# Reordering the first four units of a fused linear attention and FFN: operands of the bonus product, masks, and the release of row transfers

## Chip, cores and metric

The kernel runs on one core of a Trainium2 chip. The time is device microseconds of the whole launch; a run of it is compared with runs of the other kernel on the same chip.

## What is computed

The reference has two stages. The first is a linear attention with a decaying state for 4 batches, 8 heads, 768 steps and a head width of 48. The second is an FFN with a SiLU that takes the attention's output as 3072 tokens of 384 columns.

```python
for t in range(S):
    cur = np.einsum('bhd,bhe->bhde', u[None] * kt, vt)
    y[:, :, t] = np.einsum('bhd,bhde->bhe', rt, state + cur)
    state = w[None, :, :, None] * state + np.einsum('bhd,bhe->bhde', kt, vt)
x = y.transpose(0, 2, 1, 3).reshape(B * S, H * D)
h = x @ w_in                       # 384 -> 2048
out = (h / (1 + exp(-h))) @ w_out  # 2048 -> 384
```

All inputs and the output are float32. The decay w lies between 0.85 and 0.95 for each head and column.

## The kernel before

The 768 steps are cut into six chunks of 128, so with four batches there are 24 units (`unit`: chunk, batch). Units 0 to 3 are the first chunk of the four batches, 4 to 7 the second, and so on. Each unit loads r, k and v as 128 steps by 8 heads by 48 columns of float32 (192 KB, `ld`, line 71, on the queue of SyncE). The tiles `rin`, `kin`, `vin` have eight buffers each. The heads of r and k are padded from 48 to 64 columns of zero, by VectorE for the first four buffers and by ScalarE in `pads` for the other four.

A unit goes through these steps, named as in the order string:

- `T`: TensorE transposes r and k into a PSUM tile (`att`, two of them used in turn), line 251. `rT`, `kT`: VectorE multiplies by powers of the decay, line 257.
- `A01`, `A23`, ...: `product_pair`, line 284, the products of the decayed k and r for two units.
- `am`: VectorE masks these, line 291 (`maskM` for even units, `maskX` for odd ones).
- `ku`, `ru`, `rd`, `vu`: the term with u. GpSimd forms k*u (line 211), r*(k*u) (line 215), VectorE sums over the columns of a head (line 224), and GpSimd multiplies v by the sum (line 229).
- `v16`: ScalarE casts v, with two more copies for odd units (lines 238 to 242). `kc`: GpSimd decays k for the state (line 219). `r16`: cast of the decayed r for units of later chunks.
- `Y`, `S`: TensorE's products for the output and the state (lines 306, 318). `y16`: VectorE adds vu (line 334). `st`, `sd`, `stb`: state, its decay and its half-precision copy.
- `yT`, `xT`: TensorE turns the output, ScalarE copies it into `xT` (lines 372, 376), the input of the FFN. From unit 6 on a DMA transpose does that.
- `L`, `G` and `H`: pieces of the first FFN matmul and its SiLU (lines 387, 395). `L0.4` is the piece of batches 0 and 1 that begins at block 4 of 16 of the 2048 columns, `L2.` that of batches 2 and 3, `L4.` those of all four. The second FFN matmul is at line 408.
- `i_q0` to `i_q3`, `i_o0` to `i_o3`: requests of a quarter of `w_in` and `w_out`, on GpSimd's queue (lines 84, 89). They cast to half precision on the way. `i_q0` holds blocks 0 to 3, and so on.
- `lr`, `lk`, `lv`: loads of r, k, v of a unit. A number ahead of a star, as in `4*T0`, puts so many filler matmuls (`spin`, line 161) ahead of a step on TensorE.

Nothing reorders the program: each engine runs its instructions in the order in which they are written, with a semaphore wait where data or a buffer isn't ready. For units 0 to 5 and part of 6 and 7 the order is written out by hand in the string `order` (lines 485 to 496), after the loads of units 0 to 3 (lines 103 to 115). The loads of units 4 to 7 stand at the string's beginning, those of units 8 and 9 behind it. After that a loop (line 518) takes two units at a time and puts pieces of the FFN between their steps (`fill`); here the term with u is formed by `bonus_products`.

Of the kernel before, what the change touches and what calls it, by code (L numbers as in the profile page):

```python
# [8 lines left out]
FP = mybir.dt.float32  # L9
F16 = mybir.dt.float16  # L10
AF = mybir.ActivationFunctionType
ALU = mybir.AluOpType
# [3 lines left out]
def kernel(  # L16
# [11 lines left out]
    nc = tc.nc  # L28

    B, H, S, D = r.shape  # L30
# [10 lines left out]
    NIN = 8  # L41
# [4 lines left out]
    wrk = ctx.enter_context(tc.tile_pool(name="wrk", bufs=2))  # L46
# [3 lines left out]
    def unit(i):  # L50
        return divmod(i, B)
# [9 lines left out]
    u_bc = cst.tile([128, H, D], FP)  # L61
    rin = [big.tile([128, H, 64], FP, name=f"rin{i}") for i in range(NIN)]
    kin = [big.tile([128, H, 64], FP, name=f"kin{i}") for i in range(NIN)]
    vin = [big.tile([128, H, D], FP, name=f"vin{i}") for i in range(NIN)]
    kc = [big.tile([128, H, 64], F16, name=f"kc{i}") for i in range(NIN)]
    st = [big.tile([PR, NP, PW], FP, name=f"st{b}") for b in range(B)]
# [4 lines left out]
    def ld(i, dst, src, eng=nc.sync):  # L71
        sc, b = unit(i)
        eng.dma_start(
            out=dst[i % NIN][:, :, 0:D],
            in_=src[b, :, sc * C:sc * C + C, :].rearrange("h t d -> t h d"))

    def load(i):
        if i >= NU:
            return
        for dst, src in ((rin, r), (kin, k), (vin, v)):  # L80
            ld(i, dst, src)
# [29 lines left out]
                                            ap=[[0, 128], [D, H], [1, D]]))  # L111
    ld(0, vin, v)
    ld(1, vin, v)
    load(2)
    load(3)
    nc.vector.memset(ones, 1.0)
    for i in range(B):
        nc.vector.memset(rin[i][:, :, D:64], 0.0)
# [1 line left out]
    for b in range(B):  # L120
# [13 lines left out]
        out=maskM, in_=maskM, compare_op=ALU.is_ge, fill=0.0,  # L134
# [10 lines left out]
    eK = cst.tile([PR, NP, C], FP)  # L145
    lamR = cst.tile([PR, NP, C], FP)
    lamK = cst.tile([PR, NP, C], FP)
    lnw_bc = cst.tile([128, HD], FP)
    lamC = cst.tile([128, H, D], FP)
    wCT = cst.tile([PR, NP], FP)  # L150

    def pads():
        for i in range(B, NIN):
            for dst in (rin, kin):
                nc.scalar.copy(out=dst[i][:, :, D:64],
                               in_=idle[:, 0:128].rearrange("p (h d) -> p h d", h=H))

    def spin(n):
        zs = ps.tile([128, 512], FP, name="zs", tag="moe", bufs=4)
        for _ in range(n):  # L160
            nc.tensor.matmul(zs, idle[:, 0:128], idle, start=True, stop=True)
# [40 lines left out]
    def L(i):  # L202
        return live.setdefault(i, {})

    def bonus_products(i):
        bonus_ku(i)
        bonus_rku(i)

    def bonus_ku(i):
        L(i)["ku"] = wrk.tile([128, H, D], FP, name="ku")  # L210
        nc.gpsimd.tensor_tensor(out=L(i)["ku"], in0=kin[i % NIN][:, :, 0:D], in1=u_bc, op=ALU.mult)  # L211

    def bonus_rku(i):
        L(i)["rku_f"] = wrk.tile([128, H, D], FP, name="rku_f")
        nc.gpsimd.tensor_tensor(out=L(i)["rku_f"], in0=rin[i % NIN][:, :, 0:D], in1=L(i)["ku"],  # L215
                                op=ALU.mult)

    def decayed_k(i):
        nc.gpsimd.tensor_tensor(out=kc[i % NIN][:, :, 0:D], in0=kin[i % NIN][:, :, 0:D],  # L219
# [246 lines left out]
    def piece(word, f):  # L466
# [4 lines left out]
        "lnw": powers_r, "eK": exponents_k, "lamK": powers_k,  # L471
        "wb": spread_w,
        "lnwb": ln_w, "lamC": powers_c, "mx": cross_mask, "pads": pads, "clear": clear,
    }
    unit_steps = {
# [2 lines left out]
        "am": masked, "v16": cast_v, "kc": decayed_k,  # L478
        "vu": bonus_v,
        "Y": outputs_y, "S": outputs_s, "y16": evict_y, "yT": turn_y, "xT": copy_x,  # L480
        "st": state, "stb": state16, "ku": bonus_ku, "ru": bonus_rku, "rd": bonus_sum,
        "r16": cast_r, "sd": decayed_state, "i_q": ld_win, "i_o": ld_wout,
        "lr": lambda i: ld(i, rin, r), "lk": lambda i: ld(i, kin, k), "lv": lambda i: ld(i, vin, v),
    }
    order = """
        lnw eK lamK mx clear lr4 lk4 lv4 lr5 lk5 lv5 lr6 lk6 lv6 lr7 lk7 lv7 4*T0 ku0 rT0 kT0
        1*T1 rT1 kT1 v160 ru0 rd0 ku1 v161 3*A01 wb ru1 am0 rd1 vu0 lnwb i_q0 lamC pads am1 vu1
        4*Y0 y160 T2 kT2 2*Y1 y161 ku2 ru2 rT2 yT0 xT0 i_q1 yT1 xT1 v162 T3 kT3 rT3 ku3 ru3 rd2
        v163 4*A23 vu2 i_q2 rd3 vu3 am2 am3 L0.0 G0.0 L0.2 G0.2 Y2 y162 Y3 y163 kc0 yT2 xT2 L0.4
        G0.4 kc1 yT3 xT3 L0.6 G0.6 S0 st0 kc2 T4 kT4 rT4 kc3 L2.0 G2.0 S1 L2.2 G2.2 st1 ku4 v164  # L490
        L2.4 G2.4 S2 L2.6 G2.6 st2 ru4 i_q3 r164 L4.8 G4.8 S3 L4.9 G4.9 st3 rd4 ku5 L4.10 G4.10
        T5 kT5 rT5 L4.11 G4.11 vu4 ru5 i_o0 A45 rd5 am4 r165 v165 L4.12 G4.12 vu5 kc4 L4.13
        G4.13 am5 sd4 kc5 Y4 S4 y164 st4 L4.14 G4.14 sd5 i_o1 Y5 S5 y165 st5 L4.15 G4.15 yT4 xT4
        yT5 xT5 T6 kT6 rT6 ku6 ru6 i_o2 H0 H1 v166 r166 H2 H3 T7 kT7 rT7 ku7 i_o3 v167 r167 H4
        ru7 rd6 stb4 stb5
    """
    for word in order.split():
        if "*" in word:
# [19 lines left out]
    for i in range(B + 2, NU, 2):  # L518
# [3 lines left out]
        if i > B + 2:  # L522
            for n in nxt:
                bonus_products(n)
                decayed_k(n)
        if i > B + 2:
            masked(i)
            masked(i + 1)
        else:
            bonus_v(i)  # L530
            decayed_k(i)
            decayed_state(i)
            masked(i)
            bonus_sum(i + 1)
            masked(i + 1)
            bonus_v(i + 1)
            decayed_k(i + 1)
            decayed_state(i + 1)
            for n in nxt:
                bonus_products(n)  # L540
                decayed_k(n)
# [60 lines left out]
```

## Time and profile before

| | |
|---|---|
| median of 7 runs | 195.01 us (194.65 to 197.19) |
| profiled execution, its time | 194.78 us |
| its span, first to last instruction | 193.1 us |
| mean granted clock of TensorE | 0.991 |
| busy: PE, PEld | 184.1, 118.1 us |
| busy: DVE, ACT, POOL | 102.8, 108.3, 120.3 us |
| filler matmuls before the loop | 18 |

PE is TensorE's matmuls, PEld its weight loads, DVE VectorE, ACT ScalarE, POOL GpSimd, SP SyncE. A line of the timeline has the start in us, the duration, the engine, the line of the program, the operation, and out<-in with the shapes; in brackets stand the idle time before it and what ended it. A line of a stage has its bounds, its length, and the busy time of each engine with the number of instructions, then the granted clock as a fraction, the mean busy share of the DMA engines and GB/s. In the page, one digit stands for one of 40 equal slices of the span, 4.83 us each.

### The profile page before, as it was taken

The page shows a single profiled execution, that of the slowest core. Times are in us where ns is not written, and L with a number is a line of the kernel's source. Part 1 is how long each engine was busy: PE and PEld are TensorE (multiplying, and loading weights), DVE is VectorE, ACT ScalarE, POOL GpSimd, SP SyncE. Part 2 cuts the span into 40 slices and gives each one's busy share as a digit, 9 for nine tenths or more (in the row PEclk, how much of TensorE's full clock was granted, in tenths as well). Part 3 has the DMA queues.
Part 4 walks back from the last instruction along what each step waited for, and adds up shares of the span by engine and source line. Part 5 has one row for each costly group of instructions (what it writes and reads, how often), then busy time and mean ns, then how long its engine had stood idle before and what let it go on. Part 6 is the DMA issues. An engine that isn't in the chain of part 4 may idle for free.

```text
span 193.1 us, 5626 instructions
## 1 busy us (share of the span) xinstructions
PE 184.1 (95%) x2306; PEld 118.1 (61%) x2306; DVE 102.8 (53%) x188; ACT 108.3 (56%) x212; POOL 120.3 (62%) x159
## 2 busy tenths in 40 slices
PE   7888899989999999999999999999999999999994
PEld 2544684667766886665556665566655656644563
DVE  6577769764782682672672673673574364200120
ACT  5398277759371493076792176791376781089300
POOL 8299994999999939929829839839837430000000
PEclk9996999999999999999999999999999999999999
DMA  5999979899949559249259278177287101320022
GB/s 99 208 186 164 229 139 182 130 206 220 186 112 176 176 112 196 65 106 208 58 106 202 64 158 192 25 138 171 61 179 171 40 5 44 82 81 0 3 81 82
DMA packets 90267, 24.35 MB, mean 126 GB/s; under 512 B 83329, under 2 KB 90242, under 8 KB 90242
## 3 DMA queue, kind: packets, MB, share of 16 engines
q1 hardware_dynamic: 85136, 20.59, 49.2%
q0 software_dynamic: 3712, 3.15, 10.8%
q10 hardware_dynamic: 1394, 0.26, 0.7%
q8 instruction: 18, 0.29, 0.7%
q14 instruction: 7, 0.06, 0.1%
HBM read 20.65 MB, written 4.72 MB: 131 GB/s over the span
## 4 chain that ended last, share of the span: by engine, by line
PE 76%; POOL 12%; issue 4%; DMA 3%; ACT 2%; SPq 1%; DVE 1%; POOLq 0%
PE ops L408 31%; PE hps L387 27%; PE att L284 7%; PE att L251 4%; POOL ku L211 3%; POOL kc L219 3%; DMA u_bc<-in_u_dram 3%; POOL rku_f L215 2%; POOL vu L229 2%; PE yp L306 2%; PE yp L301 2%; POOL win L84 2%; PE sp L318 1%; PE ops L433 1%; ACT gT L395 1%
## 5 line engine op out<-in xcount | busy, mean ns | idle before, releaser
L387 PE MATMUL hps<-xT,win 128*128 128x512 f16 (+1 forms) x360 | 68.2, 337 | 0.7 <-ACT xT L376 0.5
L395 ACT ACTIVATE gT<-hps 128x512 f16<-128x512 f32 x96 | 56.2, 598 | 20.9 <-PE hps L387 18.8
L408 PE MATMUL ops<-wout,gT 128*128 128x384 f16 x368 | 64.0, 326 | 0.0
L408 PEld LDWEIGHTS <-gT 128*128 128x128 f16 x368 | 34.6, 98 | 22.2
L387 PEld LDWEIGHTS <-win 128*128 128x128 f16 x360 | 33.2, 98 | 24.3 <-issue 1.1
L229 POOL TENSOR_TENSOR vu<-vin,rku 128x384 f32<-128x384 f32 x24 | 19.8, 830 | 27.0 <-DVE rku L224 27.0
L414 ACT COPY osb<-ops 128x384 f32<-128x384 f32 x20 | 9.6, 478 | 43.4 <-PE ops L408 43.4
L291 DVE TENSOR_TENSOR am<-att,maskM 128x1024 f16<-128x1024 f32 x12 | 14.7, 1224 | 32.2 <-PE att L284 32.2
L211 POOL TENSOR_TENSOR ku<-kin,u_bc 128x384 f32<-128x384 f32 x24 | 24.1, 1005 | 4.9 <-DMA u_bc<-in_u_dram 3.3
L215 POOL TENSOR_TENSOR rku_f<-rin,ku 128x384 f32<-128x384 f32 x24 | 24.1, 1003 | 1.7
L219 POOL TENSOR_TENSOR kc<-kin,lamC 128x384 f16<-128x384 f32 x24 | 23.9, 1000 | 0.0
L284 PEld LDWEIGHTS att<-rT,kT 48*64 48x64 f32 x768 | 17.8, 134 | 6.5 <-issue 3.9
L257 DVE TENSOR_TENSOR rT<-att,lamR 112x512 f32<-112x512 f32 x24 | 16.4, 685 | 9.6 <-ACT gT L395 4.0
L284 PE MATMUL att<-rT,kT 48*64 48x128 f32 (+1 forms) x768 | 20.2, 248 | 1.0 <-DVE rT L257 0.8
L334 DVE TENSOR_TENSOR y<-yp,vu 128x384 f16<-128x384 f32 x24 | 13.3, 556 | 13.6 <-issue 4.8
L257 DVE TENSOR_TENSOR kT<-att,lamK 112x512 f32<-112x512 f32 x24 | 16.4, 682 | 4.1 <-PE att L251 4.1
L291 DVE TENSOR_TENSOR am<-att,maskX 128x1024 f16<-128x1024 f32 x12 | 14.6, 1214 | 0.0
L224 DVE TENSOR_REDUCE rku<-rku_f 128x8 f32<-128x384 f32 x24 | 12.4, 544 | 3.6 <-POOL rku_f L215 3.6
L238 ACT CAST v<-vin 128x384 f16<-128x384 f32 x24 | 11.4, 511 | 3.4 <-DMA vin<-in_v_dram 3.3
L329 POOL TENSOR_TENSOR sdec<-st,wCT 112x384 f32<-112x384 f32 x16 | 13.2, 825 | 0.0
L272 ACT CAST rT<-rT 112x512 f16<-112x512 f32 x20 | 12.4, 619 | 0.3 <-DVE rT L257 0.2
L306 PEld LDWEIGHTS <-am 128*128 128x128 f16 x192 | 9.7, 97 | 4.4 <-DVE am L291 2.9
(64 smaller groups left out, 161.7 us busy)
## 6 DMA issues: line engine op xcount, KB each, us to landing
rin<-in_r_dram SPq DMA_DIRECT2D x24, 192.0 KB, 4.2
vin<-in_v_dram SPq DMA_DIRECT2D x24, 192.0 KB, 4.1
kin<-in_k_dram SPq DMA_DIRECT2D x23, 192.0 KB, 4.1
out_dram<-osb SPq DMA_DIRECT2D x23, 192.0 KB, 2.2
win<-in_moe_w_in_dram POOLq DMA_DIRECT2D x4, 384.0 KB, 6.9
wout<-in_moe_w_out_dram POOLq DMA_DIRECT2D x4, 384.0 KB, 6.3
xT<-y SPq DMA_TRANSPOSE x18, 2.3
kin<-in_k_dram ACTq DMA_DIRECT2D x1, 192.0 KB, 4.0
```

What stands on the lines that cost most here:

```text
L211: nc.gpsimd.tensor_tensor(out=L(i)["ku"], in0=kin[i % NIN][:, :, 0:D], in1=u_bc, op=ALU.mult)
L215: nc.gpsimd.tensor_tensor(out=L(i)["rku_f"], in0=rin[i % NIN][:, :, 0:D], in1=L(i)["ku"], op=ALU.mult)
L219: nc.gpsimd.tensor_tensor(out=kc[i % NIN][:, :, 0:D], in0=kin[i % NIN][:, :, 0:D], in1=lamC, op=ALU.mult)
L229: nc.gpsimd.tensor_tensor(out=L(i)["vu"], in0=vin[i % NIN], in1=L(i)["rku"].unsqueeze(2).broadcast_to([128, H, D]), op=ALU.mult)
L257: nc.vector.tensor_tensor(out=L(i)[key].rearrange("p g (y t) -> p y g t", y=2), in0=L(i)["t"][0:PR, :, x], in1=lam.rearrange("p g (y t) -> ...
L284: nc.tensor.matmul(a[e][o0:o0 + HC, j, p, c0:C], kT[r0:r0 + D, p, s0:s0 + HC], rT[r0:r0 + D, p, c0:C], start=True, stop=True)
L291: nc.vector.tensor_tensor(out=am.rearrange("p h g c -> p (h g) c"), in0=L(i)["a"].rearrange("p h g c -> p (h g) c"), in1=(maskX if crossed ...
L306: nc.tensor.matmul(L(i)["y"][:, h, :], L(i)["am"][:, j, p, :], L(i)["vy"][:, h, :], start=not sc, stop=(not sc or j == 1))
L334: nc.vector.tensor_tensor(out=L(i)["y16"], in0=L(i)["y"], in1=L(i)["vu"], op=ALU.add)
L387: nc.tensor.matmul(hps[:, f, :], win[:, q, (ft + f) * 128:(ft + f + 1) * 128], xts[sc][:, q, b0:b0 + nb, :].rearrange("p b t -> p (b t)"), ...
L395: nc.scalar.activation(out=gts[sc][:, ft:ft + m, b0 * C:(b0 + nb) * C], in_=hpss[b0, ft], func=AF.Silu)
L408: nc.tensor.matmul(opss[b], gts[sc][:, ft, b * C:(b + 1) * C], wout[:, ft, :], start=(ft == 0), stop=(ft == NFT - 1))
```

## The change

1. The term with u of every unit is formed as r*k first and that times u afterwards. Both products stay on GpSimd. In the order string `ku` becomes `rk`.
2. In the prologue, r and k of units 2 and 3 are requested ahead of v of units 2 and 3.
3. The order of the first four units is written anew. `rk0 rk1 ru0 ru1` come first on GpSimd; `am0` stands ahead of `rd1`; `vu1` stands ahead of `i_q0`; `rT2` stands ahead of `y161`; T3 and A23 stand ahead of `yT1`; `v162`, `v163` and `pads` stand ahead of `xT1`; `i_q2` comes behind `kc0`. The 18 fillers are dealt out differently.
4. The loads of units 4 to 7 leave the string's beginning. Each unit's three loads are now behind a small GpSimd memset into the buffer that r will fill (`hold_rows`), so that the first of them waits until GpSimd has come that far. The holds stand behind `i_q0` (by way of `rk2` and `ru2`), `i_q2`, `i_q3` and `i_o0`.

```diff
-    load(2)
-    load(3)
+    for dst, src in ((rin, r), (kin, k)):
+        ld(2, dst, src)
+    for dst, src in ((rin, r), (kin, k)):
+        ld(3, dst, src)
+    ld(2, vin, v)
+    ld(3, vin, v)
...
+    def hold_rows(i):
+        nc.gpsimd.memset(rin[i][:, :, 0:4], 0.0)
...
-        nc.gpsimd.tensor_tensor(out=L(i)["ku"], in0=kin[i % NIN][:, :, 0:D], in1=u_bc, op=ALU.mult)
+        nc.gpsimd.tensor_tensor(out=L(i)["rk"], in0=kin[i % NIN][:, :, 0:D],
+                                in1=rin[i % NIN][:, :, 0:D], op=ALU.mult)
...
-        nc.gpsimd.tensor_tensor(out=L(i)["rku_f"], in0=rin[i % NIN][:, :, 0:D], in1=L(i)["ku"],
-                                op=ALU.mult)
+        nc.gpsimd.tensor_tensor(out=L(i)["rku_f"], in0=L(i)["rk"], in1=u_bc, op=ALU.mult)
...
-        lnw eK lamK mx clear lr4 lk4 lv4 lr5 lk5 lv5 lr6 lk6 lv6 lr7 lk7 lv7 4*T0 ku0 rT0 kT0
-        1*T1 rT1 kT1 v160 ru0 rd0 ku1 v161 3*A01 wb ru1 am0 rd1 vu0 lnwb i_q0 lamC pads am1 vu1
-        4*Y0 y160 T2 kT2 2*Y1 y161 ku2 ru2 rT2 yT0 xT0 i_q1 yT1 xT1 v162 T3 kT3 rT3 ku3 ru3 rd2
-        v163 4*A23 vu2 i_q2 rd3 vu3 am2 am3 L0.0 G0.0 L0.2 G0.2 Y2 y162 Y3 y163 kc0 yT2 xT2 L0.4
-        G0.4 kc1 yT3 xT3 L0.6 G0.6 S0 st0 kc2 T4 kT4 rT4 kc3 L2.0 G2.0 S1 L2.2 G2.2 st1 ku4 v164
-        L2.4 G2.4 S2 L2.6 G2.6 st2 ru4 i_q3 r164 L4.8 G4.8 S3 L4.9 G4.9 st3 rd4 ku5 L4.10 G4.10
-        T5 kT5 rT5 L4.11 G4.11 vu4 ru5 i_o0 A45 rd5 am4 r165 v165 L4.12 G4.12 vu5 kc4 L4.13
...
+        lnw eK lamK mx clear 4*T0 rk0 rT0 kT0 1*T1 rT1 kT1 rk1 ru0 rd0 v160 v161 3*A01 wb am0
+        ru1 vu0 rd1 am1 vu1 lnwb lamC i_q0 1*Y0 y160 T2 kT2 rT2 2*Y1 rk2 1*yT0 xT0 ru2 hold4 lr4
+        lk4 lv4 3*T3 kT3 rT3 v162 y161 rk3 i_q1 3*A23 v163 pads yT1 xT1 ru3 rd2 vu2 rd3 vu3 am2
+        am3 L0.0 G0.0 L0.2 G0.2 Y2 y162 Y3 y163 kc0 i_q2 hold5 lr5 lk5 lv5 yT2 xT2 L0.4 G0.4 kc1
+        yT3 xT3 L0.6 G0.6 S0 st0 kc2 T4 kT4 rT4 kc3 L2.0 G2.0 S1 L2.2 G2.2 st1 rk4 v164 L2.4
+        G2.4 S2 L2.6 G2.6 st2 ru4 i_q3 hold6 lr6 lk6 lv6 r164 L4.8 G4.8 S3 L4.9 G4.9 st3 rd4 rk5
+        L4.10 G4.10 T5 kT5 rT5 L4.11 G4.11 vu4 ru5 i_o0 hold7 lr7 lk7 lv7 A45 rd5 am4 r165 v165
...
```

From `L4.12` on the string is the same, but for `rk` in the place of `ku`.

More of the change, by code (lines that the diff above doesn't have):

```diff
@@ L205, in bonus_products, with bonus_rk @@
     def bonus_products(i):
-        bonus_ku(i)
+        bonus_rk(i)
         bonus_rku(i)
-    def bonus_ku(i):
-        L(i)["ku"] = wrk.tile([128, H, D], FP, name="ku")
-        nc.gpsimd.tensor_tensor(out=L(i)["ku"], in0=kin[i % NIN][:, :, 0:D], in1=u_bc, op=ALU.mult)
+    def bonus_rk(i):
+        L(i)["rk"] = wrk.tile([128, H, D], FP, name="rk")
+        nc.gpsimd.tensor_tensor(out=L(i)["rk"], in0=kin[i % NIN][:, :, 0:D],
+                                in1=rin[i % NIN][:, :, 0:D], op=ALU.mult)
     def bonus_rku(i):
         L(i)["rku_f"] = wrk.tile([128, H, D], FP, name="rku_f")
-        nc.gpsimd.tensor_tensor(out=L(i)["rku_f"], in0=rin[i % NIN][:, :, 0:D], in1=L(i)["ku"],
-                                op=ALU.mult)
+        nc.gpsimd.tensor_tensor(out=L(i)["rku_f"], in0=L(i)["rk"], in1=u_bc, op=ALU.mult)
     def decayed_k(i):
@@ L480 @@
         "Y": outputs_y, "S": outputs_s, "y16": evict_y, "yT": turn_y, "xT": copy_x,
-        "st": state, "stb": state16, "ku": bonus_ku, "ru": bonus_rku, "rd": bonus_sum,
-        "r16": cast_r, "sd": decayed_state, "i_q": ld_win, "i_o": ld_wout,
+        "st": state, "stb": state16, "rk": bonus_rk, "ru": bonus_rku, "rd": bonus_sum,
+        "r16": cast_r, "sd": decayed_state, "i_q": ld_win, "i_o": ld_wout, "hold": hold_rows,
         "lr": lambda i: ld(i, rin, r), "lk": lambda i: ld(i, kin, k), "lv": lambda i: ld(i, vin, v),
@@ L485 @@
     order = """
-        lnw eK lamK mx clear lr4 lk4 lv4 lr5 lk5 lv5 lr6 lk6 lv6 lr7 lk7 lv7 4*T0 ku0 rT0 kT0
-        1*T1 rT1 kT1 v160 ru0 rd0 ku1 v161 3*A01 wb ru1 am0 rd1 vu0 lnwb i_q0 lamC pads am1 vu1
-        4*Y0 y160 T2 kT2 2*Y1 y161 ku2 ru2 rT2 yT0 xT0 i_q1 yT1 xT1 v162 T3 kT3 rT3 ku3 ru3 rd2
-        v163 4*A23 vu2 i_q2 rd3 vu3 am2 am3 L0.0 G0.0 L0.2 G0.2 Y2 y162 Y3 y163 kc0 yT2 xT2 L0.4
-        G0.4 kc1 yT3 xT3 L0.6 G0.6 S0 st0 kc2 T4 kT4 rT4 kc3 L2.0 G2.0 S1 L2.2 G2.2 st1 ku4 v164
-        L2.4 G2.4 S2 L2.6 G2.6 st2 ru4 i_q3 r164 L4.8 G4.8 S3 L4.9 G4.9 st3 rd4 ku5 L4.10 G4.10
-        T5 kT5 rT5 L4.11 G4.11 vu4 ru5 i_o0 A45 rd5 am4 r165 v165 L4.12 G4.12 vu5 kc4 L4.13
-        G4.13 am5 sd4 kc5 Y4 S4 y164 st4 L4.14 G4.14 sd5 i_o1 Y5 S5 y165 st5 L4.15 G4.15 yT4 xT4
-        yT5 xT5 T6 kT6 rT6 ku6 ru6 i_o2 H0 H1 v166 r166 H2 H3 T7 kT7 rT7 ku7 i_o3 v167 r167 H4
-        ru7 rd6 stb4 stb5
+        lnw eK lamK mx clear 4*T0 rk0 rT0 kT0 1*T1 rT1 kT1 rk1 ru0 rd0 v160 v161 3*A01 wb am0
[5 more added lines that the diff above has]
+        L4.10 G4.10 T5 kT5 rT5 L4.11 G4.11 vu4 ru5 i_o0 hold7 lr7 lk7 lv7 A45 rd5 am4 r165 v165
+        L4.12 G4.12 vu5 kc4 L4.13 G4.13 am5 sd4 kc5 Y4 S4 y164 st4 L4.14 G4.14 sd5 i_o1 Y5 S5
+        y165 st5 L4.15 G4.15 yT4 xT4 yT5 xT5 T6 kT6 rT6 rk6 ru6 i_o2 H0 H1 v166 r166 H2 H3 T7
+        kT7 rT7 rk7 i_o3 v167 r167 H4 ru7 rd6 stb4 stb5
     """
```

## The prediction

> **What bounds the kernel now.** I read the slices first, then busy time by stage, then the chain of waits, then the timeline of 5 to 40 us and the landing of single transfers.
>
> ```profile
> PEclk9996999999999999999999999999999999999999
> DMA  5999979899949559249259278177287101320022
> ```
>
> ```profile
> 12.40:15.80 3.40, 2.14 (x37) 1.25 (x37) 3.18 (x6) 3.37 (x12) 3.38 (x5) 1.00 0.73 134
> 15.80:19.20 3.40, 3.31 (x27) 1.60 (x28) 2.38 (x5) 2.63 (x6) 3.22 (x5) 0.52 1.15 181
> 19.20:22.60 3.40, 3.30 (x85) 2.81 (x84) 2.31 (x3) 0.95 (x2) 3.38 (x5) 0.97 1.26 226
> ...
> 50.00:60.00 10.00, 10.00 (x114) 6.63 (x113) 6.31 (x13) 4.48 (x10) 9.84 (x13) 1.00 0.68 136
> ```
>
> The columns are PE, PEld, DVE, ACT, POOL, granted clock, DMA share, GB/s. From 50 us on PE is never idle for long, so what the first 50 us save or lose moves the end one for one. Before that PE idles about 6 us (10.00 less busy time, summed over the five stages of 10 us), and runs one stretch at half clock around 15.8 to 19.2. POOL is nearly full from 8.5 us on, and DMA is nearly full up to 48 us: who gets the transfers first matters more than how many there are.
>
> ```profile
> 8.46 1.00 POOL L211 TENSOR_TENSOR ku<-kin,u_bc 128x384 f32<-128x384 f32 x1 [3.34 <-DMA u_bc<-in_u_dram]
> ...
> 11.05 1.21 DVE L291 TENSOR_TENSOR am<-att,maskM 128x1024 f16<-128x1024 f32 x1
> ...
> 20.72 1.21 PEld L387 LDWEIGHTS <-win 128*128 128x128 f16 x12
> ...
> 23.92 0.83 PE L387 MATMUL hps<-xT,win 128*128 128x256 f16 x6
> ...
> 29.55 0.99 POOL L211 TENSOR_TENSOR ku<-kin,u_bc 128x384 f32<-128x384 f32 x1 [0.54 <-DMA kin<-in_k_dram]
> ```
>
> ```profile
> 37.94 0.97 POOL kc L219
> ...
> 38.96 0.34 PE sp L318 x4
> ```
>
> POOL stands 3.34 us waiting for u. The masks am0 and am1 follow (11.05, 13.09), then the turns of units 2 and 3, A23 (19.14), the first FFN pieces (L0.0 at 20.72), am2, am3, and L0.4 at 23.92. From 25.78 (st0) DVE is dense to 34.06 (rT5); A45, the y products and S5 follow it, and the last two lines, from the chain of waits, show S5 start as POOL's kc5 ends. Numbers in brackets are idle time and what ended it.
>
> ```profile
> win<-in_moe_w_in_dram POOLq DMA_DIRECT2D x1, 384.0 KB, 7.0
> ...
> win<-in_moe_w_in_dram POOLq DMA_DIRECT2D x1, 384.0 KB, 6.8
> ...
> vin<-in_v_dram SPq DMA_DIRECT2D x1, 192.0 KB, 4.1
> ...
> vin<-in_v_dram SPq DMA_DIRECT2D x1, 192.0 KB, 10.2
> ...
> kin<-in_k_dram SPq DMA_DIRECT2D x1, 192.0 KB, 8.7
> ```
>
> The last column is us from issue to landing. These are issues at 13.31, 17.10, 12.73, 15.73 and 20.80: weight part 0 lands at 20.3, part 1 at 23.9 (just when L0.4 starts), v3 at 16.8, v4 at 25.9, k5 at 29.5.
>
> **What the Trainium skill says.** *DMA: Bandwidth & Descriptors*, "Anatomy of one DMA": a wait is held by the issuing sequencer, not by the DMA engine. So lr4 behind its hold stops SP and all that follows; SP waiting for compute is in this trace (4.3 us at most for an osb of ACT). "Queues, rings and completion order": each DMA engine takes turns between the queues with work. The trace agrees: rows beside weights take up to 10.2 us, rows alone 3.7 to 4.4. *TensorE: Matmul & The Clock Gate*, "Part 1": after an idle window of about 3.4 us the clock is halved for at least such a window; the 0.52 of 15.8 to 19.2, after a window with 2.14 us of PE work in 3.40, agrees. *GPSIMD Engine Reference*, 3.1: a product of two inputs is bound by the read port, whichever the inputs are; here 1005 ns (ku) and 1003 ns (rku_f).
>
> **The change, part by part.**
>
> *r by k first.* No product is added. rk0 can start when k0 has landed (1.42 + 4.0 = 5.4), rk1 when k1 has (2.52 + 4.4 = 6.9), so both are done by 8.0. u lands at 8.3: ru0 8.45 to 9.45, ru1 to 10.5. The four products end at 10.5 instead of 12.58. For later units r lands before k, so the other operand costs nothing.
>
> *Masks.* A01 ends at 10.42 as before. rd0 is out of the way by 10.05, so am0 runs 10.5 to 11.7, rd1 to 12.2, am1 12.1 to 13.3 (before 14.3): 1.0 us sooner. vu1 waits for rd1 until 12.2 and ends at 13.05, ahead of weight request 0, which therefore leaves at about 13.05, only 0.25 sooner.
>
> *Order of units 2 and 3.* The queue's slots keep their landings (13.65, about 14.3, 15.1, 16.8); they now carry r3, k3, v2, v3. On PE: Y0 11.8, T2 12.1, Y1 13.35, yT0 13.85 (y160 ends 13.8), three fillers, T3 14.8 to 15.5. DVE: kT2, rT2 to 15.05, kT3, rT3 to 16.85. A23 then runs 16.9 to 18.55 instead of 19.14 to 20.79. There are 18 fillers before and after, so they cost nothing in sum.
>
> *What is late next.* yT1 is done at 18.9, but ACT now has v162, v163 and the pads ahead of xT1. v3 lands at 16.8; v163 to 17.4, two crossed copies of 0.51 to 18.4, eight pads at 0.2 (14.04 to 15.73 before) to 20.05, xT1 to 20.5. So L0.0 starts at 20.5, 0.2 sooner, and most of A23's 2.2 us is eaten. The masks use the rest: ru3 ends on POOL at 18.85, rd3 19.4, am2 to 20.55, am3 to 21.7 (before 23.2). L0.0 and L0.2 end at 22.0, Y3 at 22.6, y162 at 22.9, yT2 at 23.2 and L0.4 starts at 23.1 to 23.2: 0.75 sooner.
>
> *Weights and held rows.* Demand from the page: queue 1's 49.2% of 193.1 us is 95 us for 85136 packets, so a row load of 1024 packets (8 heads by 128 rows) takes 1.14 us of all engines; queue 0's 10.8% is 20.9 us for eight parts, 2.6 us each. From 16.8 to 25.9 three row loads (3.4 us) went beside weights, so rows got about 0.38 and weights 0.62 when both run. With rows of unit 4 issued at 16.1 (hold4) and about 2.4 us until they move, part 0 lands at 18.5 to 19.2 and part 1 (asked at 17.05) at about 23.2, 0.7 sooner: just enough for L0.4. r4 and k4 get 0.38 from 18.5: r4 21.5, k4 about 24.3, against 22.55 before. T4 is due at 24.9 instead of 25.68: enough, by 0.6. Part 2 (asked at 21.5, 0.75 later) lands near 27.7, due 28.7. Unit 5, released at about 22.4, has k5 near 29.8; T5 is due at 31.1, and POOL idles 2.2 us after that product anyway. Units 6 and 7 (released 28.2, 34.7) are due at 39.5 and 43.5; I put k7 at 41 to 42.5. All of it is the same demand in another order, so the last rows (v9, 53.6) move by the idle of the engines only, some 0.6 us, which T9 and its casts hide.
>
> *The holds themselves.* A memset of 128 x 32 isn't in the trace; the nearest row is 0.15 us for a kc memset of 128 x 128. Bounds: 0.05 and 0.25 each; I take 0.15, for four 0.6 us. Below nothing is excluded, since POOL is in order. hold5 and hold6 lie in POOL's slack before vu4 (2.24 us of idle at 30.54). hold7 lies in the dense stretch from vu4 (32.82) to kc5 (38.9) which S5 waits for at 38.96: it costs 0.15.
>
> *Sum.* 0.75 at L0.4 and st0 carries through the dense DVE stretch, less 0.15 before S5: 0.6 us. The profiled execution took 194.78 with a span of 193.1, so 1.7 lie around it; the span becomes 192.5, that execution 194.2. The median of the runs is 0.23 above the profiled one: 194.4.
>
> **The rivals.**
>
> *A larger gain.* If v3 lands 0.5 sooner (slot 5's 15.1 plus 1.14 undisturbed) and ACT works faster through its copies, L0.0 no longer waits for xT1 and only am3 at 21.7 decides: yT2 22.4, L0.4 22.5, 1.4 us sooner, if part 1 is there. For: part 0 and part 1 have fewer rivals. Against: eight pads in front of xT1. Time 193.6 (194.78 - 1.4 + 0.23); a shorter cold stretch could add up to the 1 us that cold fillers now cost, 192.6.
>
> *The clock falls elsewhere.* PE now idles from 18.9 to 20.5; with 0.8 us of idle before A23 the window 15.9 to 19.3 holds about 2.2 us of work, as the one before the cold stretch now did. L0.0 and L0.2 at half rate cost 12 x (213 - 123 ns) = 1.1 us (213: 256 columns at half of 2.4 GHz, the clock page's price, an estimate; 123: 1.48 / 12). The gain becomes a loss of 0.35: 195.4, at worst 196.
>
> *Rows of unit 4 late.* The loss decides from k4 after 25.5 on, where PE stands in T4 with L2.0 and the later pieces behind it. The hold issues k4 at 16.9; with the longest landing seen (10.2) it is there at 27.1, 1.4 us after T4's old start, and DVE's slack then no longer hides it: a loss of 0.8 to 1.5, with a halved clock after so long a wait up to 2.7. Time 195.0 + 1.4 = 196.4. For: DMA is full and weights take 0.62 of it. Against: only one row load is ahead of k4.
>
> *The change doesn't act.* If L0.4 waits for part 1 until 23.9 as before, the time stays at 195.0; I count it with the forecast.
>
> **How the numbers follow.** Forecast 0.46, larger gain 0.22, clock 0.18, late rows 0.14. A measurement of this kernel tells about 1% from no change, so bounds are 193.06 and 196.96. Faster by over 1%: 0.12 of the larger gain and 0.03 of the forecast's own error, 0.15. Slower by over 1%: 0.07 of the late rows, 0.03 of the clock, and 0.03 of the forecast where rows of units 7 or 9 stall T7 or T9, 0.13. Within: 0.72. The range runs from the larger gain with a saved cold stretch (192.7) to the late rows (196.4).
>
> **What would show it.** Right: rk0 near 5.5, am1 ends near 13.3, A23 starts near 17, L0.0 waits for xT of ACT near 20.5, L0.4 near 23.2 and S5 near 38.4. Wrong: PE waiting in T4 for kin; a clock below 1 at 19 to 23; L0.4 waiting for win; S5 no sooner than 38.96.

## The result, and the profile after

The changed kernel is slower: 198.55 us in the median of 12 runs (196.43 to 200.08) against 195.53 of the kernel before in the same sessions. The ratio is 1.0128, with a 95% interval of 1.0089 to 1.0166. Ratios are formed without disturbed runs (over 1.5% above the fastest of the same kernel), medians over all of them, so the two need not agree. The profiled execution took 198.29 us with a span of 196.6, 3.5 more than the span before. The forecast was 194.4, with a range of 192.7 to 196.4.

The slices of the changed kernel, first the granted clock, then the DMA share. In the lines shown below, the line numbers of the steps in runs of the changed kernel are higher by 7 than before.

```profile
PEclk9999889999999999999999999999999999999999
DMA  5999999099966939438439258339269111320022
```

Busy time by stage, with the same columns as before (PE, PEld, DVE, ACT, POOL, clock, DMA share, GB/s):

```profile
12.40:15.80 3.40, 3.31 (x46) 1.64 (x42) 2.92 (x5) 2.57 (x5) 3.30 (x4) 1.00 0.76 129
15.80:19.20 3.40, 2.48 (x69) 1.78 (x67) 2.16 (x5) 0.00 (x0) 3.38 (x6) 1.00 1.15 191
19.20:22.60 3.40, 0.00 (x0) 0.10 (x1) 2.44 (x3) 2.93 (x10) 3.25 (x6) 1.00 1.23 218
22.60:26.00 3.40, 2.68 (x16) 1.95 (x16) 0.00 (x0) 1.26 (x4) 3.40 (x4) 0.53 1.06 159
```

Up to 18.5 us the new order works, and the half-rate stretch at 15.8 is gone. Then PE stands still for a whole stage (19.2 to 22.6, busy 0.00) while ScalarE works; in the stage before that, it was ScalarE that had nothing to do (0.00). The half-rate stretch comes at 22.6 instead (clock 0.53). The timeline says who waits for what:

```profile
5.51 1.00 POOL L218 TENSOR_TENSOR rk<-kin,rin 128x384 f32<-128x384 f32 x1 [0.39 <-DMA kin<-in_k_dram]
...
12.02 1.22 DVE L298 TENSOR_TENSOR am<-att,maskX 128x1024 f16<-128x1024 f32 x1
...
16.72 1.55 PE L291 MATMUL att<-rT,kT 48*64 48x128 f32 x60 [0.27 <-DVE rT L264]
...
19.61 0.51 ACT L245 CAST v<-vin 128x384 f16<-128x384 f32 x1 [3.92 <-DMA vin<-in_v_dram]
...
22.80 0.47 ACT L383 COPY xT<-yT 128x384 f16<-128x384 f16 x1
...
23.32 2.72 PE L394 MATMUL hps<-xT,win 128*128 128x256 f16 x12 [4.77 <-ACT xT L383]
...
27.25 0.82 PE L394 MATMUL hps<-xT,win 128*128 128x256 f16 x6
```

The first three lines are the gains, as forecast. The fourth is the loss: ScalarE stands 3.92 us in v163, waiting for v3. Behind it in ScalarE's queue stand two crossed copies, eight pads and xT1, and L0.0 on PE waits for xT1. The chain of waits holds the transfer itself, and further on S5:

```profile
12.78 6.81 DMA vin<-in_v_dram
...
42.32 0.34 PE sp L325 x4
```

v3 was requested at 12.78, as before (12.73), but took 6.81 us to land where it took 4.1. L0.4 is 3.33 us later than before (27.25 against 23.92), S5 3.36 (42.32 against 38.96): nothing up to there wins it back.

### The profile page after: what moved, and what is told of

It is laid out like the page before. It is cut to its first block, busy times and chain, and to the rows that moved or that the text cites. A ratio compares the mean times of both kernels' runs of the same rounds, so it can differ in the third digit from the quotient of the medians.

```text
span 196.6 us, 5631 instructions
## 1 busy us (share of the span) xinstructions
PE 183.9 (94%) x2306; PEld 118.5 (60%) x2306; DVE 102.7 (52%) x188; ACT 108.6 (55%) x212; POOL 120.5 (61%) x163
## 4 chain that ended last, share of the span: by engine, by line
PE 75%; POOL 7%; SPq 6%; issue 5%; DMA 3%; ACT 2%; DVE 1%; POOLq 0%
PE ops L415 31%; PE hps L394 26%; PE att L291 7%; SPq L73 5%; PE att L258 4%; DMA vin<-in_v_dram 3%; POOL kc L226 3%; PE yp L313 2%; PE yp L308 2%; PE sp L325 1%; PE ops L440 1%; POOL vu L236 1%; ACT gT L402 1%; POOL rku_f L223 1%; POOL win L84 1%
## 5 line engine op out<-in xcount | busy, mean ns | idle before, releaser
L394 PE MATMUL hps<-xT,win 128*128 128x512 f16 (+1 forms) x360 | 69.4, 342 | 5.5 <-ACT xT L383 5.3
L394 PEld LDWEIGHTS <-win 128*128 128x128 f16 x360 | 33.8, 99 | 29.6 <-issue 5.0
L218 POOL TENSOR_TENSOR rk<-kin,rin 128x384 f32<-128x384 f32 x24 | 24.1, 1004 | 1.8 <-DMA kin<-in_k_dram 1.7
L223 POOL TENSOR_TENSOR rku_f<-rk,u_bc 128x384 f32<-128x384 f32 x24 | 23.9, 999 | 2.0 <-DMA u_bc<-in_u_dram 0.4
L226 POOL TENSOR_TENSOR kc<-kin,lamC 128x384 f16<-128x384 f32 x24 | 23.9, 1000 | 0.0
L341 DVE TENSOR_TENSOR y<-yp,vu 128x384 f16<-128x384 f32 x24 | 13.3, 556 | 18.3 <-PE yp L313 8.1
L291 PE MATMUL att<-rT,kT 48*64 48x128 f32 (+1 forms) x768 | 20.5, 248 | 1.3 <-DVE rT L264 1.0
L423 DVE COPY osb<-ops 128x384 f32<-128x384 f32 x3 | 1.7, 557 | 19.8 <-PE ops L415 19.8
```

What stands on the lines that cost most here:

```text
L218: nc.gpsimd.tensor_tensor(out=L(i)["rk"], in0=kin[i % NIN][:, :, 0:D], in1=rin[i % NIN][:, :, 0:D], op=ALU.mult)
L223: nc.gpsimd.tensor_tensor(out=L(i)["rku_f"], in0=L(i)["rk"], in1=u_bc, op=ALU.mult)
L291: nc.tensor.matmul(a[e][o0:o0 + HC, j, p, c0:C], kT[r0:r0 + D, p, s0:s0 + HC], rT[r0:r0 + D, p, c0:C], start=True, stop=True)
L341: nc.vector.tensor_tensor(out=L(i)["y16"], in0=L(i)["y"], in1=L(i)["vu"], op=ALU.add)
L394: nc.tensor.matmul(hps[:, f, :], win[:, q, (ft + f) * 128:(ft + f + 1) * 128], xts[sc][:, q, b0:b0 + nb, :].rearrange("p b t -> p (b t)"), ...
```

## Experiments

Two theories were to be told apart. Theory A: v3 lands late behind weight part 0, and ScalarE's new order makes L0.0 wait for it. Theory B: the held rows of units 4 to 7, or the clock by itself. Edits are shown as pieces of the order string; a ratio is to the kernel before, with its 95% interval.

**ScalarE's order put right, on the changed kernel.**

```diff
-3*T3 kT3 rT3 v162 y161 ... 3*A23 v163 pads yT1 xT1
+3*T3 kT3 rT3 v162 pads y161 ... 3*A23 yT1 xT1 v163
```

> Edit: on ScalarE the pads stand right behind v162 and xT1 stands ahead of v163; nothing else differs from the changed kernel. Theory A (v3 lands late behind weight part 0, and ScalarE's order turns this into the wait of L0.0): v3 still lands near 19.5, but L0.0 starts near 19.4, as part 0 lands, instead of 23.3; L0.4 then starts near 23.7, when part 1 lands; 3 to 4 us faster than the changed kernel, 194 to 195. Theory B (the held rows of units 4 to 7 or the clock itself make the loss): PE's wait moves to T4 or the later rows, and the time stays above 197.

Measured: 195.25 us, 0.9985 (0.9947 to 1.0022). The whole loss is gone, with the holds and the requests as they are. The execution that was profiled was the longest of the 14 (196.85) and had an extra wait (T2 for k2, 1.8 us), so its L0.0 at 22.81 doesn't show the forecast 19.4; a later run with this order and an earlier weight request 1 comes near it (19.56). There is no gain over the kernel before either.

> Edit: only the pads move, to behind v162; v163 stays ahead of xT1. Theory A: xT1 starts as soon as v163's three copies are done, near 21.2 instead of 22.8, so L0.0 is 1.6 us sooner; the time falls by 1.6 us or somewhat more where the clock's half-rate window then covers less. If v3's landing had no part in it, xT1 would follow A23 at once, near 18.6, and this run would equal the one with xT1 first.

```diff
-3*T3 kT3 rT3 v162 y161 ... 3*A23 v163 pads yT1 xT1
+3*T3 kT3 rT3 v162 pads y161 ... 3*A23 v163 yT1 xT1
```

Measured: 196.73 us, 1.0067 (1.0040 to 1.0094). Moving the pads alone takes about half of the loss away. xT1 started at 21.67, 1.13 sooner than in the changed kernel, 1.6 us behind the start of v163's cast. The expected 21.2 was missed, and this trace doesn't show v3's part: here v2 came late (v162's cast at 18.06), the pads followed, and v163's cast behind them began about a microsecond after v3 was there.

**v3's wait taken out.** Unit 3's cast reads unit 2's tile; the transfer of v3 stays.

```diff
-        nc.scalar.copy(out=v16, in_=vin[i % NIN])
+        nc.scalar.copy(out=v16, in_=vin[2 if i == 3 else i % NIN])
```

> Edit: the changed kernel, in which unit 3's cast reads unit 2's v; v3 is still loaded, at the same place, and is read by vu3, so only ScalarE's wait for it goes. Left out is unit 3's own v in the matmul part. Theory A: the cast starts behind v162 at 15.7, pads end near 18.8, xT1 starts at 18.8 and L0.0 near 19.4 as part 0 lands; 2.5 to 3.5 us faster than the changed kernel. If v3's landing isn't what ScalarE's chain hangs on, the time stays above 197.5.

Measured: 195.42 us, 1.0007 (0.9972 to 1.0043). With ScalarE's order, the pads, the holds and all requests of the changed kernel, taking that one wait away removes the loss. Its groups of waits on PE, in us in total, times and longest, have xT1's wait at 0.6 instead of 4.8:

```profile
PE hps L394 <- ACT xT L383: 1.1, 2, 0.6
```

L0.0 came at 21.57, not 19.4, since k2 held T2 up for 1.1 us in this execution and the cast of v2 was late. So it is the time that shows the step, not that mark.

**Weight part 0 later, on the changed kernel.**

```diff
-lnwb lamC i_q0 1*Y0 y160 T2 kT2 rT2 2*Y1 rk2 1*yT0
+lnwb lamC 1*Y0 y160 T2 kT2 rT2 2*Y1 rk2 i_q0 1*yT0
```

> Edit: weight request 0 is issued behind rk2, about 1 us later than in the changed kernel (near 14 instead of 12.95); ScalarE's order stays. Theory A: v3's packets are through before part 0 moves, v3 lands at 16.3 to 16.9, xT1 starts near 20.1 and L0.0 near 20.6, or when part 0 lands (near 20.5); the time falls by 2 to 3 us. If v3 is late for another reason (its place in SyncE's queue), it still lands near 19.5 and the time stays or gets worse.

Measured: 196.15 us, 1.0038 (1.0012 to 1.0063). v3 is there when v162 is done:

```profile
14.73 0.93 POOL L84 DMA_DIRECT2D win<-in_moe_w_in_dram  x1
...
16.80 0.93 ACT L245 CAST v<-vin 128x384 f16<-128x384 f32 x2
```

So v3's place in SyncE's queue is not what makes it late. The ratio falls from 1.0128 to 1.0038, which is about 1.8 of the 2.5 us lost. What keeps the rest isn't shown: in the profiled execution T2 waited 1.5 us for k2, and part 0 itself is later.

**The holds.** First taken out of the changed kernel, then put alone into the kernel before.

```diff
-ru2 hold4 lr4 lk4 lv4 ... i_q2 hold5 lr5 lk5 lv5 ... i_q3 hold6 lr6 lk6 lv6 ... i_o0 hold7 lr7 lk7 lv7
+mx clear lr4 lk4 lv4 lr5 lk5 lv5 lr6 lk6 lv6 lr7 lk7 lv7 ... ru2 ... i_q2 ... i_q3 ... i_o0
```

> Edit: the four holds are taken out and the loads of units 4 to 7 stand at the order's beginning again, as in the kernel before; all else is the changed kernel. Theory A: v3 still lands near 19 to 19.5, since its place and the time of weight request 0 are the same, and the time stays within 0.5 us of the changed kernel's, perhaps slower as the weights share with more rows. Theory B (holds make the loss): the time falls back to 195.

Measured: 197.62 us, 1.0080 (1.0047 to 1.0113): still slower than before, the interval overlapping that of the changed kernel. v163's cast began at 19.18, xT1 at 22.36.

> Edit: the kernel before with only the four holds (behind ru2, i_q2, i_q3 and i_o0) and the loads of units 4 to 7 moved behind them. Theory A: no part of the loss comes from here; within 0.8 us of before, with T4 still in time. Theory B (held rows starve T4 or later turns): slower by 1.5 us or more, with PE waiting in a turn of units 4 to 7.

```diff
-mx clear lr4 lk4 lv4 ... ku2 ru2 rT2 ... vu2 i_q2 ...
+mx clear ... ku2 ru2 hold4 lr4 lk4 lv4 rT2 ... vu2 i_q2 hold5 lr5 lk5 lv5 ...
```

Measured: 195.01 us, 0.9980 (0.9953 to 1.0006): nothing. Theory B's first half falls: held rows starve no turn (from 22 us on PE waits for no row load). Here too v3 was late (cast at 20.29) and it cost nothing; in the old order xT1 doesn't stand behind it.

**r by k and the masks alone, on the kernel before.**

```diff
-4*T0 ku0 rT0 kT0 1*T1 rT1 kT1 v160 ru0 rd0 ku1 v161 3*A01 wb ru1 am0 rd1 vu0 lnwb i_q0 lamC pads am1 vu1
+4*T0 rk0 rT0 kT0 1*T1 rT1 kT1 rk1 ru0 rd0 v160 v161 3*A01 wb am0 ru1 vu0 rd1 am1 vu1 lnwb lamC i_q0 pads
```

> Edit: the kernel before with only r by k first, both r-k products ahead of the two products with u, and vu1 ahead of weight request 0; loads, holds and the order of TensorE, ScalarE and VectorE as before. Theory A: weight request 0 leaves near 13.0 as in the changed kernel, so v3 may land at 19 to 19.5, but here xT1 doesn't stand behind it, and only Y3 needs v163, near 21: the time is within 1 us of before, 194.4 to 195.5. If an early weight request alone does the harm, it is slower by 2 us or more.

Measured: 195.59 us, 0.9984 (0.9952 to 1.0017). L0.0 ran at 19.35, 1.4 us sooner than before, but L0.4 at 23.34, held up by the transfer of part 1:

```profile
23.34 0.83 PE L387 MATMUL hps<-xT,win 128*128 128x256 f16 x6 [0.94 <-DMA win<-in_moe_w_in_dram]
```

**ScalarE's order and the time of part 0, on the kernel before.** These four runs set the two factors apart from all other parts of the change.

```diff
 # ScalarE's order
-lamC pads am1 ... yT1 xT1 v162 ... rd2 v163 4*A23
+lamC am1 ... yT1 v162 ... rd2 v163 pads xT1 4*A23
 # part 0 sooner
-rd1 vu0 lnwb i_q0
+rd1 lnwb i_q0 vu0
 # part 0 later
-lnwb i_q0 ... y161 ku2 ru2
+lnwb ... y161 ku2 i_q0 ru2
```

> Edit: the kernel before with only ScalarE's order changed: v163 and the pads ahead of xT1. v3 should land near 16.8 as before, so that xT1 starts near 20.1 and L0.0 near 20.6 to 21: within 0.5 us of before. This tells whether the order does harm by itself, or only together with the late landing of v3. If it alone costs over 2 us, the landing had no part in it.

> Edit: the kernel before with only weight request 0 ahead of vu0, some 0.8 us sooner; ScalarE's order as before. v3 lands late, near 19.5, but only Y3 needs it, at 21 to 22, so the time is within 0.6 us of before. If the late v3 alone costs, it is slower by 2 us.

> Edit: the kernel before with ScalarE's new order (v163 and the pads ahead of xT1) and weight request 0 ahead of vu0, some 0.8 us sooner; no other part of the change. If the loss is the two together, v3 lands near 19.5 or later, xT1 starts at 22.5 to 23, L0.0 near 23, and the time is 197.5 to 199, all of the changed kernel's loss from these two edits. If other parts of the change are needed for the loss, it stays below 196.5.

> Edit: the kernel before with ScalarE's new order, and weight request 0 behind ku2, near 15.3 instead of 13.3. v3's request then leads by 2 us or more: v3 lands near 16.5, xT1 starts near 20 and L0.0 at 21 to 22, when part 0 lands; the time is within 1 us of before and spreads less than with ScalarE's order alone. If ScalarE's order is what costs, it is 197 or more.

| on the kernel before | ratio (95%) | median us |
|---|---|---|
| ScalarE's order alone | 0.9999 (0.9951 to 1.0047) | 196.59 |
| part 0 sooner alone | 0.9995 (0.9957 to 1.0034) | 194.68 |
| both | 1.0156 (1.0104 to 1.0207) | 198.50 |
| order, and part 0 later | 1.0078 (1.0051 to 1.0105) | 196.43 |

The medians of the kernel before were 195.18 beside the first run and 195.01 beside the other three. Part 0 sooner costs nothing by itself. Together with ScalarE's order it costs as much as the whole change (six runs), without r by k, without holds and without the new order of the first loads.

ScalarE's order alone is less clear than its ratio. Six of its 14 runs took 197.48 to 199.76 us, as long as the changed kernel's, and don't enter the ratio; the median of all 14 is 1.4 us above that of the kernel before. In the execution that was profiled (195.34) v3 came in time. v3's request leads by little in this run (0.49 us, see below), so v3 may have been late in the six, but no trace of one was kept, and this isn't shown.

In the profiled execution of both together v163's cast began at 18.91 and xT1 at 22.10, but L0.0 waited until 23.30 for A23, which ran at half clock behind a late k3 (T3's second half at 18.10): k3 was late as well as v3, so this run mixes two waits. With part 0 later, v3 came at 16.57 and xT1 at 19.76 as expected, and then L0.0 waited for part 0 instead, 1.70 us, and ran at half clock. That may be where its 0.78% comes from. The loss of 1.4 us by the medians is more than the 1 us expected at most; the spread is smaller, as expected (195.54 to 198.18).

**The clock's part.**

```diff
-am2 am3 L0.0 G0.0
+am2 am3 12*L0.0 G0.0
```

> Edit: the changed kernel with 12 filler matmuls on TensorE ahead of L0.0 (2.6 us at full clock, inside the wait for xT1 from 18.6 to 23.3). This separates the clock's part from the wait's: if the half-rate stretch at 22.6 to 26.0 is made by the wait and costs 1 us, L0.0 and L0.2 take 1.5 instead of 2.5 us and the time falls by about 1 us; L0.0 still starts near 23.3. If the clock has no part, the time stays within 0.3 us of the changed kernel's.

Measured: 197.47 us, 1.0094 (1.0058 to 1.0131), an interval that overlaps the changed kernel's. In the profiled execution, the longest of the 13 (198.95), the fillers ended near 21.0, PE idled another 2.46 us, and the clock fell all the same (0.56 in the stage from 22.6 to 26.0; L0.0 and L0.2 took 2.72 us as in the changed kernel).

The mean granted clocks of the single runs say more. In six of the 13 the clock stayed at 0.999 or 1.0, so there was no half-rate stretch. These took 195.78 to 197.47 us, 196.52 in the median, against 195.16 for the 27 runs of the kernel before beside them that had a clock of 0.998 or more. So without any half-rate stretch about 1.4 us of loss are left: the clock by itself doesn't make it, and Theory B's second half falls too. The clock adds to it: the six runs at 0.991 have a median of 197.88. In the changed kernel no run kept the full clock: nine of 12 had 0.983, and three had 0.991, the profiled one among them. Of 213 runs of the kernel before beside the experiments, only ten were as low as 0.982. By an estimate from its stage at 0.53, a half-rate stretch of 3.4 us takes 0.008 off the mean of a 196.6 us span, so the nine had about two such stretches and the profiled one had one.

**Towards a better version.** With v3 and xT1 put right, part 1's landing was next, so it was requested sooner.

```diff
 # on the run with ScalarE's order put right
-rk2 1*yT0 xT0 ru2 hold4 ... rk3 i_q1 3*A23
+rk2 i_q1 1*yT0 xT0 ru2 hold4 ... rk3 3*A23
```

> Edit: the run with pads early and xT1 ahead of v163, and weight request 1 issued two GpSimd products sooner (behind rk2). If L0.4 is now bound by part 1's landing near 23.7, as in the changed kernel's trace, part 1 lands near 22.2 to 22.7 and L0.4 starts 1 us sooner: 194.2 to 194.7 where its parent has 195.25. If the rest of the gain is lost elsewhere (T2 waiting for k2, the clock), the time stays within 0.4 of the parent's.

Measured: 193.79 us, 0.9939 (0.9912 to 0.9966), faster than both kernels and than expected. In the profiled execution the first pieces are free of xT1, and the mean clock was 1.00:

```profile
18.36 0.48 ACT L383 COPY xT<-yT 128x384 f16<-128x384 f16 x1 [1.46 <-PE yT L379]
18.79 0.51 ACT L245 CAST v<-vin 128x384 f16<-128x384 f32 x1
...
19.56 1.48 PE L394 MATMUL hps<-xT,win 128*128 128x256 f16 x12 [1.24 <-DMA win<-in_moe_w_in_dram]
...
22.15 0.82 PE L394 MATMUL hps<-xT,win 128*128 128x256 f16 x6
```

> Edit: the run with part 1 sooner (pads early, xT1 ahead of v163, weight request 1 behind rk2), now without the four holds, the loads of units 4 to 7 at the beginning. If holding rows back is worth something once ScalarE's order is right, this is slower than its parent by 0.3 to 1 us, since parts 0 and 1 then move beside more rows; if weights win the DMA engines anyway, it equals its parent within 0.3.

The same without the four holds (the edit is that of the changed kernel without holds): 194.19 us, 0.9961 (0.9936 to 0.9987). The intervals overlap, so a worth of the holds isn't shown.

> Edit: the kernel before with only weight request 1 moved ahead of ku2, some 2 us sooner. There L0.4 at 23.9 is bound by part 1 and by am3, Y3 and y162 alike, so I expect no gain: within 0.5 us of before, the later ku2 perhaps costing a little. If the earlier request alone gains 1 us or more, r by k and the earlier masks are worth nothing in the best version.

```diff
-y161 ku2 ru2 rT2 yT0 xT0 i_q1 yT1
+y161 i_q1 ku2 ru2 rT2 yT0 xT0 yT1
```

Measured: 194.88 us, 0.9995 (0.9970 to 1.0020): on the kernel before the sooner request of part 1 gains nothing. In its trace Y3 waits for am3 (0.76 us), and L0.4 follows at 24.48. So the gain needs other parts of the change as well; which of them (products, masks, the order of units 2 and 3) wasn't separated.

## Why the prediction was wrong

**The step that failed** is "the queue's slots keep their landings (13.65, about 14.3, 15.1, 16.8)". v2, in the third, was there at 15.2 as forecast; v3, in the fourth, landed at 19.6 instead of 16.8. I saw that weight request 0 leaves 0.25 us sooner (it was 0.36) and put the cost of this at nothing. The packets of the two queues in half a microsecond show what it costs (q1: rows, q0: weights; packets, MB, share of the engines). Before, from 16.0 and from 16.5:

```profile
q0 software_dynamic: 45, 0.05, 102.4%
q1 hardware_dynamic: 199, 0.04, 38.3%
...
q0 software_dynamic: 72, 0.07, 89.6%
q1 hardware_dynamic: 43, 0.01, 15.1%
```

After, from 14.0 (rows alone), from 15.5 and from 16.0:

```profile
q1 hardware_dynamic: 610, 0.11, 113.4%
...
q0 software_dynamic: 38, 0.04, 75.6%
q1 hardware_dynamic: 147, 0.03, 35.8%
...
q0 software_dynamic: 58, 0.06, 70.7%
q1 hardware_dynamic: 54, 0.01, 18.9%
```

Rows alone move about 600 packets in 0.5 us; beside weights it is 43 to 84 until most of part 0 is through (18.0). My share of 0.38 was a mean over a stretch with gaps between the weight parts; while a part moves, rows move about a tenth of these packets. So what is left of v3 when part 0 starts waits for nearly all of part 0. Part 0's packets start half a microsecond sooner after the change, and v3 falls on the wrong side. The lead of v3's request over part 0's tells the two sides apart in nine executions whose timelines show both requests:

| lead of v3's request over part 0's, us | v163's cast starts |
|---|---|
| 1.83 (order, part 0 later) | 16.57 |
| 0.58 (before) | 17.2, v3 there at 16.8 |
| 0.49 (order alone) | 16.51 |
| 0.40 (r by k and masks alone) | 19.50 |
| 0.36 (before, part 1 sooner) | 18.12 |
| 0.17 (changed kernel) | 19.61 |
| -0.33 (holds alone) | 20.29 |
| -0.44 (part 0 sooner alone) | 19.22 |
| -1.10 (both) | 18.91 |

Eight more executions, read from the views of the DMA, fit: with a lead of 1.2 us (part 0 later on the changed kernel) v3 landed at 16.6, with leads of 0.40 to -1.15 at 17.7 to 19.7. So in all 17 the edge lies between 0.49 and 0.40 us; how late v3 is beyond it varies from 17.7 to 20.3. Each is one execution of one kernel.

**The sum, with what was measured.** v163 to xT1: forecast 3.25 us (16.8 to 20.05), measured 3.19 (19.61 to 22.80); right. v3: 2.8 later; L0.0 therefore at 23.32 instead of 20.5. The half-rate stretch that I had kept as a rival came too, in the gap before L0.0. From L0.0 to Y2, before and after:

```profile
20.73 1.48 PE L387 MATMUL hps<-xT,win 128*128 128x256 f16 x12
22.13 0.37 PE L306 MATMUL yp<-v,am 128*128 128x48 f16 x8
...
25.83 0.52 PE L313 MATMUL yp<-v,am 128*128 128x48 f16 x8
```

After the change L0.0 starts at 23.32, so the way to Y2 takes 2.51 us instead of 1.40, 1.1 more (forecast 1.1). Against the kernel before: L0.0 2.6 later, 1.1 for the clock, and 0.4 back between Y2 and L0.4, where Y3 no longer waits for am3: 3.3 at L0.4.

**Right**, by its marks: rk0 at 5.51 (5.5), am1's end at 13.24 (13.3), A23's end at 18.3 (18.55), holds of 0.12 to 0.14 us (0.15), part 1 at 23.65 (23.2). "What is late next" named the right wait, L0.0 for xT1 behind v163 and the pads. k4 landed at 22.9, not 24.3, so the rival with late rows of unit 4 had nothing to stand on. "If L0.4 waits for part 1 until 23.9 as before, the time stays at 195.0": this fits the runs without the loss (0.9985 and 0.9984; in the second, L0.4 is seen waiting for part 1), so the 0.6 us of gain was not there either.

**Two readings were loose.** Rows alone took up to 4.6 us (v2, 9.05 to 13.65), not 4.4. And the window that I took as idle ahead of the half-rate stretch held 2.14 us of PE work in 3.40. After the change one with 2.48 was followed by a clock of 1.00 and one with no work by 0.53, so how much work keeps the clock up isn't shown.

**The mistake in judgement.** The path from v3 to L0.0 had no slack in my own sum, and all of it hung on one landing in a DMA that I had described as nearly full. The bounds of that landing belonged in the range: 16.3, and 22.9 by the 10.2 us seen for v4. With 3.7 us behind them they give 20.0 to 26.6 for L0.0.

## What to carry to other kernels

When a step is put on a queue behind a transfer that it doesn't need, its slack becomes that transfer's slack: ask of every word moved on an in-order engine which landing it now waits for. A request for wide weights that leaves a few tenths of a microsecond sooner can push a transfer of short rows back by nearly the time of the weight part (here 2.8 us), so don't place work that others need behind the last row load ahead of such a request. Then look for the next transfer before counting a gain: here the new order gained nothing, even with ScalarE's order put right, until part 1 was asked for sooner.

## What the runs showed of the hardware

Beside one weight request, loads of 192-byte rows fell from about 600 packets in 0.5 us to 43 to 84. In 17 executions v3 landed at 16.5 to 16.8 us where its request led the weight request by 0.49 us or more (four of them), and at 17.7 to 20.3 where it led by 0.40 or less (13). Filler matmuls that ended 2.46 us before the next work did not keep the clock from falling in the execution that was profiled (0.56 in the stage after); in six of the 13 runs of that kernel the mean clock stayed at 0.999 or 1.0.
